# Strassen's scheme in the first layer of an expert FFN on one Trainium2 core: seven products in place of eight

## The chip, the core and the metric

The kernel runs on one core of a Trainium2 chip. TensorE (PE) multiplies matrices: it holds a stationary operand of 128x128, streams a moving operand past it and writes into PSUM. VectorE (DVE) and ScalarE (ACT) work on rows in SBUF and PSUM, GpSimd (POOL) on SBUF alone, SyncE (SP) issues DMAs. The metric is the device time of one execution in microseconds; the kernel before takes 1500.97 us, the median of three runs from 1498.53 to 1502.5.

## The reference

```python
# 1. attention: 4 x 8 heads, 768 steps, head size 40, a 40x40 state per head
y[t] = r[t] @ state
state = state * w[t] - (state @ a[t]) b[t] + v[t] k[t]
# 2. first FFN: x is 3072 x 320
x = (max(x @ w_in, 0) ** 2) @ w_out              # 320 -> 2048 -> 320
# 3. second FFN: 4 experts, every token goes to all of them
p = domain_probs / (domain_probs.sum(-1) + 1e-9)
out = sum over e of p[:, e] * (max(x @ w1[e], 0) @ w2[e])   # 320 -> 1024 -> 320
```

All is float32. The matmuls of the FFNs run on numbers of fewer bits (fp32r), so each operand is split into a rounded high part and a low part that is the rest; a product is made of three: high x high, high x low, low x high.

## The kernel before

The first half of the program is the attention, in 24 steps, with the first FFN beside it: 12 blocks of 256 tokens, each with 16 tiles of 128 hidden features. The order of all that is made by a list scheduler (`Schedule`) from operations with costs, due times and dependencies. Block 11 of the first FFN is written out behind it, by the list `ffn`: units (layer one of a tile) and ends (layer two), the end two tiles behind the unit. The results of a block go to DRAM (`y1d`, `y1_out`), with the last 64 of 320 features doubled on POOL (`y1_double`).

The second FFN runs over 4 experts, 12 blocks, 8 tiles of 128 hidden features: 384 items. Its input is loaded back from `y1d` (`x2_load`), transposed on PE and split by ACT and DVE (`x2_tr`, while block 11 and expert 0 run), and stays in SBUF for all experts (`x2h`, `x2l`). A tile's weights are loaded, rounded by ACT, and their low parts are made by DVE and POOL (`load_w`). An item is `ffn1`, 8 matmuls of 256 columns: 320 features are 128 + 128 + 64, three matmuls for each 128 and two for the 64, whose high and low weights share the partitions. ACT then makes the high part of the rectified result and DVE its low part (L1013, L1014); `ffn2` is 6 matmuls of 320 columns, one item later, so that PE doesn't wait for the two. After 8 items the result of a block is scaled by the token's probability and added up: by ACT for expert 0 (L995), by DVE for the others (L997). The last expert's blocks go out by SP (L999).

Each engine runs its instructions in the order of the program. PSUM has eight banks: two for layer one (`ps1`), two for transposes (`pst`), four for two blocks of layer two (`ps2`, `ps3`).

## Time and profile before

| | |
|---|---|
| three runs, median | 1500.97 us |
| the profiled execution | 1497.41 us |
| its span, first to last instruction | 1495.6 us |
| mean granted TensorE clock | 0.971 |
| busy: PE, PE weight loads | 1406.6, 1341.6 us |
| busy: DVE, ACT, POOL | 837.2, 736.6, 210.4 us |
| first and last L1013 (items of the second FFN) | 786.2, 1489.7 us |
| moved by DMA | 107.18 MB |

The span is the time from the first to the last instruction. Busy time is the union of an engine's instructions; PE's are pipelined, so a matmul's duration (0.28 us) is longer than the distance to the next one's start. "Idle before" is the time in which an engine stood still ahead of an instruction, and the arrow says what ended it.

### The profile page before, as it was taken

To read this page: it belongs to the slowest core of one execution; us is meant where nothing else is said; L and a number is where in the kernel's file an instruction comes from. 1 tells how busy PE (TensorE), PEld (TensorE's weight loads), DVE (VectorE), ACT (ScalarE), POOL (GpSimd) and SP (SyncE) were. 2 spreads that over 40 slices of the span, in tenths; PEclk is the share of its full clock that TensorE was granted. 3 is DMA by queue.
4 is the path that set the end of the run, shared out by engine and by line. 5 is a ranking of instruction groups with operands and counts; after the bars stand their busy time and mean duration, and the time that the engine had idled before them with its cause. 6 is when DMAs were issued, how large, how long until landed. Compare 5 with 4: busy or idle time off the path is not lost.

```text
span 1495.6 us, 39619 instructions
## 1 busy us (share of the span) xinstructions
PE 1406.6 (94%) x16336; PEld 1341.6 (90%) x16336; DVE 837.2 (56%) x2184; ACT 736.6 (49%) x1943; POOL 210.4 (14%) x299
## 2 busy tenths in 40 slices
PE   3788999899999999999999999999999999999998
PEld 3476889788888888888999999999999999999998
DVE  7889968778778778778443333233333333323322
ACT  5487768667677777677673333322222222222221
POOL 4121322221312312311020000000000000000000
PEclk9899989899999999999999999999999999999999
DMA  8465343342442442431141111000000000000000
GB/s 249 110 192 172 91 119 88 109 133 71 125 124 78 127 130 67 133 99 50 36 132 61 42 50 52 1 30 20 30 1 11 20 1 2 1 10 27 19 27 27
DMA packets 133909, 107.18 MB, mean 72 GB/s; under 512 B 95968, under 2 KB 108256, under 8 KB 133728
## 3 DMA queue, kind: packets, MB, share of 16 engines
q1 hardware_dynamic: 133728, 104.64, 24.6%
q8 instruction: 129, 2.11, 0.6%
q14 instruction: 52, 0.43, 0.1%
HBM read 85.34 MB, written 14.55 MB: 67 GB/s over the span
## 4 chain that ended last, share of the span: by engine, by line
PE 72%; DVE 10%; DMA 8%; ACT 5%; issue 2%; SPq 2%; POOL 1%; DVEq 0%; ACTq 0%; POOLq 0%
PE z L251 24%; PE h L251 8%; PE pz L257 8%; PE pz L260 8%; PE pz L256 8%; PE px L571 3%; PE py L260 3%; DMA td<-mu 2%; PE py L256 2%; DMA TT<-td 2%; DVE t L745 2%; PE py L257 2%; DVE tmp L742 2%; PE ptx L648 2%; DMA xr<-y 1%
## 5 line engine op out<-in xcount | busy, mean ns | idle before, releaser
L1014 DVE SCALAR_TENSOR_TENSOR zl<-z,zh 128x256 fp32r<-128x256 f32 x384 | 163.0, 424 | 466.2 <-ACT zh L1013 466.2
L1013 ACT ACTIVATE zh<-z 128x256 fp32r<-128x256 f32 x384 | 147.5, 384 | 506.6 <-PE z L251 505.0
L251 PE MATMUL z<-x2h,w 128*128 128x256 f32 x1920 | 380.8, 282 | 0.0
L251 PE MATMUL z<-x2l,w 128*128 128x256 f32 x1152 | 320.4, 278 | 0.0
L251 PEld LDWEIGHTS z<-x2h,w 128*128 128x128 f32 x1920 | 306.3, 188 | 0.0
L257 PE MATMUL pz<-w,zh 128*128 128x320 f32 x768 | 231.3, 309 | 0.0
L256 PE MATMUL pz<-w,zh 128*128 128x320 f32 x768 | 230.7, 308 | 0.0
L251 PEld LDWEIGHTS z<-x2l,w 128*128 128x128 f32 x1152 | 216.8, 188 | 0.0
L251 PE MATMUL h<-xh,w 128*128 128x256 f32 x960 | 198.1, 289 | 0.0
L260 PE MATMUL pz<-w,zl 128*128 128x320 f32 x768 | 175.0, 309 | 0.0
L251 PE MATMUL h<-xl,w 128*128 128x256 f32 x576 | 164.0, 286 | 0.7 <-DVE xl L872 0.7
L251 PEld LDWEIGHTS h<-xh,w 128*128 128x128 f32 x960 | 157.4, 193 | 2.2
L256 PEld LDWEIGHTS pz<-w,zh 128*128 128x128 f32 x768 | 144.4, 188 | 0.0
L257 PEld LDWEIGHTS pz<-w,zh 128*128 128x128 f32 x768 | 144.2, 188 | 0.0
L256 PE MATMUL py<-w,gh 128*128 128x320 f32 x384 | 127.6, 340 | 5.1 <-ACT gh L807 5.1
L812 DVE TENSOR_TENSOR gl<-r,gh 128x256 fp32r<-128x256 f32 x192 | 84.7, 442 | 78.0 <-ACT r L809 77.3
L260 PEld LDWEIGHTS pz<-w,zl 128*128 128x128 f32 x768 | 128.4, 188 | 0.0
L257 PE MATMUL py<-w,gh 128*128 128x320 f32 x384 | 118.5, 316 | 0.0
L251 PEld LDWEIGHTS h<-xl,w 128*128 128x128 f32 x576 | 111.2, 193 | 0.9 <-DVE xl L872 0.9
L804 ACT ACTIVATE r<-h 128x256 f32<-128x256 f32 x192 | 73.3, 382 | 63.7 <-PE h L251 54.9
L745 DVE TENSOR_TENSOR t<-t,tmp 128x126 f32<-128x126 f32 (+22 forms) x372 | 96.5, 259 | 6.8
L260 PE MATMUL py<-w,gl 128*128 128x320 f32 x384 | 93.7, 326 | 6.5 <-DVE gl L812 6.2
(104 smaller groups left out, 2305.7 us busy)
## 6 DMA issues: line engine op xcount, KB each, us to landing
in<-kba SPq DMA_DIRECT2D x24, 768.0 KB
raw<-wf SPq DMA_DIRECT2D x32, 352.0 KB
raw<-wm SPq DMA_DIRECT2D x32, 234.0 KB
wd<-w SPq DMA_DIRECT2D x24, 264.0 KB
rf<-rv SPq DMA_DIRECT2D x24, 256.0 KB
r<-rv SPq DMA_DIRECT2D x24, 256.0 KB
v<-rv SPq DMA_DIRECT2D x24, 256.0 KB
mu<-md SPq DMA_DIRECT2D x24, 256.0 KB
```

The source lines that it names most:

```text
L251: pe.matmul(ps, a, b, start=n == 0, stop=n == len(mm) - 1)
L256: pe.matmul(pys[tt], gh[:, sl], t[:, 256:576], start=first, stop=False)
L257: pe.matmul(pys[tt], gh[:, sl], t[:, 960:1280], start=False, stop=False)
L260: pe.matmul(pys[tt], gl[:, sl], t[:, 256:576], start=False, stop=last)
L571: pe.matmul(px[64 * j:64 * j + 64, p], t[:, 0:64], t[:, 64:168], start=True, stop=True)
L648: pe.matmul(d["ptx", h][own(h, j), p], T[i, 4 * h + p], d["x", h][i, p], start=True, stop=True)
L742: dve.tensor_tensor(v["tmp"], a, b, ALU.mult)
L745: dve.tensor_tensor(c, c, v["tmp"], ALU.subtract)
L804: act.activation(g["r"], g["ps"], AF.Relu)
L812: dve.tensor_tensor(g["gl"], g["r"], g["gh"].bitcast(F32), ALU.subtract)
L1013: act.activation(gh, ps, AF.Relu)
L1014: dve.scalar_tensor_tensor(gl, ps, 0.0, gh.bitcast(F32), ALU.max, ALU.subtract)
```

## The change

The second FFN works on pairs of blocks (512 tokens) and pairs of tiles (256 hidden features): 4 experts x 6 pairs x 4 = 96 steps. In a step layer one is a product of 2 x 2 blocks: two halves of the features (160 = 128 + 32), two of the hidden features (128), two of the tokens (256). Strassen's scheme, in Winograd's form, makes the four results out of seven products (`products`) in place of eight: each is four matmuls of 256 columns (high x high, high x low, low x high, and one for the 32 features that are left, with the parts beside each other on the partitions). The results are added up by DVE in a tile `C`, from PSUM, then rectified and split as before, with 512 columns an instruction. Layer two (`l2`, 24 matmuls of 320 columns) runs one step later.

The scheme wants four sums of the weights' blocks and four of the tokens', and the high and low parts of all seven operands. A planner (`Beside`) holds jobs with an engine, a duration, a due step and what they need, and at each step gives out jobs on each engine until a time for that engine is used up (`emit`); the times are 4.94 us of ACT, 3.19 of DVE, 3.87 of POOL and 3.0 of SP a step, and less beside block 11. Transposes (`x_block`) are given by `blocks`, at most two a step, inside `l2`. A pair's inputs are scaled by a power of two per token (`x2_big`, `x2_scale`, `x2_mul`), which the probabilities take back. The operands of the six pairs and of the sets of weights are made while block 11 and expert 0 run (experts 1 and 2 make the sets of the expert behind them), stored in DRAM by SP (`x_store`, `set_store`) and fetched by POOL's queue for the later steps (`x_fetch`, `set_fetch`). `load_w`, `x2_tr`, `y1_double` and the old loop go. Block 11's results go through DRAM like the others'.

```diff
-NF2 = 8
+NPAIR, NPW = 6, 4
...
+    def ready(self, j, n, eng):
+        _, _, _, _, _, _, deps, lag, after, _ = j
+        if n < after:
+            return False
+        for d in deps:
+            if d in self.jobs:
+                return False
+            if d in self.given:
+                at, by = self.given[d]
+                if by != eng and n < at + lag:
+                    return False
+        return True
...
+    def blocks(self, n, most):
+        while most:
+            l = sorted((j[:2], k) for k, j in self.jobs.items() if j[2] == ("pe",) and self.ready(j, n, "pe"))
+            if not l:
+                return
+            key = l[0][1]
+            j = self.jobs[key]
+            if j[9]:
+                most -= 1
+                eng = min(j[9], key=lambda e: self.used.get(e, 0))
+                self.used[eng] = self.used.get(eng, 0) + j[3]
+                self.give(key, n, eng, (self.engines[eng],))
+            else:
+                self.give(key, n, "pe")
...
+    def emit(self, n, budget):
+        left = {e: t - self.used.get(e, 0) for e, t in budget.items()}
+        while True:
+            l = []
+            for k, j in self.jobs.items():
+                for e in j[2]:
+                    if e in left and (left[e] > 0 or j[0] <= n) and self.ready(j, n, e):
+                        l.append((j[0], j[1], -left[e], e, k))
+            if not l:
+                break
+            _, _, _, e, k = min(l)
+            j = self.jobs[k]
+            left[e] -= j[3]
+            self.give(k, n, e, (self.engines[e],) if len(j[2]) > 1 or j[4].__name__ in ("x_round", "set_round", "set_round2") else ())
+        self.used = {e: -min(0, t) for e, t in left.items()}
...
-    def y1_double(k):
-        pool.tensor_copy(yy[k][:, :, 320:384], yy[k][:, :, 256:320])
+            yy[k] = buf3(f"y1_{k}", *buf)[:, 0:2 * DM].rearrange("p (c x) -> p c x", c=2)
+        act.copy(yy[k][:, t], py[k][t])
...
+    xsd = dram.tile([NPAIR, 128, 21 * 256], F32R, name="xsd", bufs=1)
+    wsd = dram.tile([NPW, 128, 31 * 128], F32R, name="wsd", bufs=1)
...
+        sp.dma_start(m.rearrange("p (c x) -> p c x", c=2)[:, :, 0:512], wf[n, :, 0:1024].rearrange("p (c x) -> p c x", c=2))
+        sp.dma_start(w, wf[n, :, 1024:1664])
...
+    def set_sum(n, o, x, y, f):
+        m = raw[n][0]
+        pool.tensor_tensor(m[:, :, o], m[:, :, x], m[:, :, y], f)
...
+    def set_round(s, i, eng):
+        m = flat(raw[s.n][0][:, i // 2])
+        h = slice(448 * (i % 2), 448 * (i % 2) + 448)
+        copy(eng, (s.a, s.b)[i // 2][:, h], m[:, h])
...
+    def set_low(s, i):
+        m = flat(raw[s.n][0][:, 0])
+        o = (s.b[:, 896:1280], s.a[:, 896:1280], s.l)[i]
+        h = slice(384 * i, min(384 * i + 384, 896))
+        minus(dve, o, m[:, h], f32(s.a[:, h]))
...
+    def set_rest(s):
+        c = flat(raw[s.n][0][64:96, 1])
+        minus(pool, c, c, f32(s.b[64:96, 0:896]))
...
+    def set_fetch(s):
+        for t, x, y in parts(s):
+            pool.dma_start(t, wsd[s.n % NPW, :, x:y])
+        slot[s.n] = s
...
+    def x2_mul(k):
+        for t in range(2):
+            y = yl[k][:, t, :, 0:160]
+            dve.tensor_scalar(y, y, inv[:, 2 * k + t:2 * k + t + 1], None, ALU.mult)
...
+        ps = pst.tile([128, 2, 2, 128], F32, tag="tr", name=f"ptr{p}_{i}")
+        for t in range(2):
+            y = yl[2 * p + k][:, t, h]
+            pe.transpose(ps[:, 0, t], y[:, 0:128], ident)
+            pe.transpose(ps[:, 1, t], y[:, 128:256], ident)
+        copy(eng, xc[p][:, :, o], ps.rearrange("p c t x -> p c (t x)"))
+
+    def x_sum(p, o, a, b):
+        r = xc[p]
+        minus(pool, r[:, :, o], r[:, :, a], r[:, :, b])
...
+        copy(eng, xs[0, p][:, o, 0:2], xc[p][:, :, o])
+
+    def x_low(p, o):
+        minus(dve, xs[0, p][:, o, 2], xc[p][:, 0, o], f32(xs[0, p][:, o, 0]))
+
+    def x_rest(p, o):
+        c = xc[p][32:64, 1, o]
+        minus(pool, c, c, f32(xs[0, p][32:64, o, 1]))
+
+    def x_done(p, o):
+        act.copy(xs[0, p][32:64, o, 1], xc[p][32:64, 1, o])
...
+    def x_store(p):
+        sp.dma_start(f32(xsd[p]), f32(xs[0, p].rearrange("p a b x -> p (a b x)")))
+
+    def x_fetch(e, p):
+        xs[e, p] = bp2.tile([128, 7, 3, 256], F32R, tag="X", name=f"X{e}_{p}")
+        pool.dma_start(xs[e, p].rearrange("p a b x -> p (a b x)"), xsd[p])
...
+        Q = [
+            (ps1 if i < 2 else pst).tile([128, 2, 256], F32, tag="l1" if i < 2 else "tr", name=f"Q{n}_{i}")
+            for i in range(4)
+        ]
+
+        def prod(i, q):
+            hi, c = v.a[:, 128 * i:128 * i + 128], v.b[:, 128 * i:128 * i + 128]
+            o = Q[q % 4][:, q // 4]
+            pe.matmul(o, hi, X[:, i, 0], start=True, stop=False)
+            pe.matmul(o, hi, X[:, i, 2], start=False, stop=False)
+            pe.matmul(o, v.low(i), X[:, i, 0], start=False, stop=False)
+            pe.matmul(o, c, X[:, i, 1], start=False, stop=True)
+            return o
+
+        C = bp.tile([128, 4, 256], F32, tag="C", name=f"C{n}")
+        c22, c12, c21, c11 = (C[:, i] for i in range(4))
+        plus = lambda o, x, y: dve.tensor_tensor(o, x, y, ALU.add)
+        g = gz[n] = {}
+
+        def relu(i, units):
+            gh, gl = low_home(n, 2 * i), low_home(n, 2 * i + 1)
+            src = C[:, 0::3] if i == 0 else C[:, 1:3]
+            act.activation(gh, src, AF.Relu)
+            for x, u in enumerate(units):
+                g[u] = gh[:, x], gl[:, x]
+            return lambda: dve.scalar_tensor_tensor(gl, src, 0.0, f32(gh), ALU.max, ALU.subtract)
+
+        act.copy(c11, prod(0, 0))
+        plus(c21, c11, prod(5, 1))
+        plus(c12, c21, prod(4, 2))
+        p7 = prod(3, 3)
+        plus(C[:, 0:3:2], C[:, 1:3], sub(p7, [[0, 2], [1, 256]]))
+        plus(c11, c11, prod(1, 4))
+        low = relu(0, ((1, 1), (0, 0)))
+        plus(c12, c12, prod(6, 5))
+        plus(c21, c21, prod(2, 6))
+        low()
+        relu(1, ((0, 1), (1, 0)))()
...
+        for t in range(4):
+            if t == 3 and hook:
+                hook()
+            sl = slice(128 * (t % 2), 128 * (t % 2) + 128)
+            for f in range(2):
+                gh, gl = g[f, t // 2]
+                hi, lo = w[:, 320 * f:320 * f + 320], w[:, 640 + 320 * f:960 + 320 * f]
+                pe.matmul(py2[0][t], gh[:, sl], hi, start=j == f == 0, stop=False)
+                pe.matmul(py2[0][t], gh[:, sl], lo, start=False, stop=False)
+                pe.matmul(py2[0][t], gl[:, sl], hi, start=False, stop=j == NPW - 1 and f == 1)
...
+        D = {0: (-51, -15, -14, -13, -11, -8, -6, -4, -4), 1: (-13, -9, -10, -8, -3, -3, -1, 1, 1)}.get(
+            P, tuple(e + d for d in (-8, -6, -5, -5, -4, -4, -2, -2, 0)))
+        ld = [job("sp", 0.45, x2_load, k + i, deps=[("blk", P - 1, 2 * i), ("blk", P - 1, 2 * i + 1)], lag=0, due=D[0], key=("ld", k + i)) for i in range(2)]
+        bg = [job("dve", 0.82, x2_big, k + i, deps=[ld[i]], lag=2 if P else 1, due=D[1]) for i in range(2)]
...
+            job("pe", 0.66, x_block, P, i, deps=free + [dup[i // 2]], due=D[4], key=("blk", P, i), via=("act", "dve") if P == 0 else ("act",))
...
+            raw_of[o] = job("pool", 1.33, x_sum, P, o, x, y, deps=blks, lag=0, due=D[5])
...
+            r = job(("act", "dve") if P == 0 else ("act",), 0.65, x_round, P, o, deps=[raw_of[o]], due=D[6], lag=0 if o in (0, 1, 6) else 1, after=NPW * (P - 1) - 1 if P else -99)
+            job("dve", 0.42, x_low, P, o, deps=[r], due=D[7], key=("low", P, o))
+            c = job("pool", 0.72, x_rest, P, o, deps=[r] + [raw_of[u] for u in users[o]], lag=0, due=D[7])
+            job("act", 0.41, x_done, P, o, deps=[c], due=D[8], key=("done", P, o))
+        job("sp", 0.45, x_store, P, deps=[(x, P, o) for x in ("low", "done") for o in range(7)], due=e + 4, after=e + 1)
...
+            b = PER * e + (0 if e == 0 else 1) + (6 if e == 0 else 2) * i
+            prev = prepare(Set(n, spare, b), tuple(b + d for d in (0, 2, 5, 1, 1)), b, ("act",), i < NPW - 1, prev)
...
+            at(post, PER * (e + 1) - NPW + i, set_fetch, Set(NPW * (e + 1) + i, homes[i - 1]))
+        homes, spare = [spare] + homes[:NPW - 1], homes[NPW - 1]
+    for G in range(NPAIR, NE * NPAIR):
+        at(post, NPW * (G - 2) + 3, x_fetch, *divmod(G, NPAIR))
...
+    light = dict(act=0.66, dve=1.22, pool=2.56, sp=2.0)
+    i = -NP
+    plan.emit(i - 1, light)
+    for g, k, f in ffn:
+        if g is moe1_end and f == NF1 - 1:
+            plan.must(0)
+            products(0, *steps[0])
+        g(k, f)
+        if g is moe1_unit and f < 2 or g is moe1_end:
+            plan.blocks(i, 2)
+            plan.emit(i, light)
+            i += 1
+    for n, s in enumerate(steps):
+        e, p, j = s
+        if n:
+            products(n, *s)
+            l2(n - 1, *steps[n - 1], lambda: plan.blocks(n, 2))
+            if j == 0:
+                l2_end(*steps[n - 1][:2])
         else:
...
+            plan.blocks(0, 2)
+        plan.emit(n, dict(act=4.94 - 2.1 * (e == j == 0), dve=3.19 - 2.1 * (e > 0 and j == 0), pool=3.87, sp=3.0))
+        run(post, n)
```

## Rows read from the trace of the kernel before

**Rows 1.** The page: busy us, share, instructions; then tenths in 40 slices.
```profile
PE 1406.6 (94%) x16336; PEld 1341.6 (90%) x16336; DVE 837.2 (56%) x2184; ACT 736.6 (49%) x1943; POOL 210.4 (14%) x299
...
PE   3788999899999999999999999999999999999998
...
DVE  7889968778778778778443333233333333323322
...
ACT  5487768667677777677673333322222222222221
...
PEclk9899989899999999999999999999999999999999
```

**Rows 2.** Windows of the second FFN: stretch, length, busy us, clock, DMA, GB/s.
```profile
800.00:820.00 20.00, 20.00 (x158) 19.99 (x157) 6.71 (x15) 8.13 (x19) 1.03 (x1) 1.00 0.13 39
...
1000.00:1100.00 100.00, 100.00 (x771) 100.00 (x771) 34.14 (x75) 25.13 (x61) 6.20 (x6) 1.00 0.07 23
```

**Rows 3.** PE in order of time, one item: start, duration in us, line, tiles.
```profile
801.23 0.28 PE L251 MATMUL z<-x2h,w 128*128 128x256 f32 x1
...
802.17 0.31 PE L256 MATMUL pz<-w,zh 128*128 128x320 f32 x1
...
803.05 0.82 PE L967 MATMUL ptr<-cs,yl 128*128 128x128 f32 x6
...
803.63 0.37 PE L251 MATMUL z<-x2h,w 128*128 128x256 f32 x1
```

**Rows 4.** Groups by line, DVE: shapes, count, busy us, mean ns, idle before.
```profile
L812 DVE TENSOR_TENSOR gl<-r,gh 128x256 fp32r<-128x256 f32 x192 | 84.7, 442 | 78.0 <-ACT r L809 77.3 <-ACT y L826 0.2
...
L536 DVE TENSOR_TENSOR xv<-pv,cs 64x512 f32<-64x512 f32 x96 | 64.2, 686 | 2.1 <-PE pv L531 0.3
...
L668 DVE TENSOR_TENSOR ys<-pys,FF 128x256 f32<-128x256 f32 x48 | 19.6, 409 | 0.0
...
L872 DVE TENSOR_TENSOR xl<-xr,xh 128x768 fp32r<-128x768 f32 x12 | 11.5, 957 | 2.6 <-ACT xh L869 1.4 <-ACT gh L807 0.5
```

**Rows 5.** Order of time, POOL and DVE early in the attention stage.
```profile
15.64 1.25 POOL L454 TENSOR_TENSOR in<-in,s 128x512 f32<-128x512 f32 x1 [0.66 <-DVE s L442]
...
15.73 1.30 DVE L306 TENSOR_SCALAR raw<-raw 128x236 uint32<-128x236 uint32 x1
...
17.14 0.39 DVE L308 SCALAR_TENSOR_TENSOR raw<-raw 128x236 uint32<-128x236 uint32 x1
...
17.46 0.27 DVE L306 TENSOR_SCALAR raw<-raw 128x234 uint32<-128x234 uint32 x1
```

**Rows 6.** One line of the inversion: durations in ns, shortest, median, longest.
```profile
L745 DVE TENSOR_TENSOR t<-t,tmp x372: 135/261/1192, 34.4 to 712.4; 128x126 f32<-128x126 f32 x18, 128x30 f32<-128x30 f32 x12, 128x56 f32<-128x56 f32 x12, 128x78 f32<-128x78 f32 x12
```

**Rows 7.** Groups by line, ACT and POOL.
```profile
L1013 ACT ACTIVATE zh<-z 128x256 fp32r<-128x256 f32 x384 | 147.5, 384 | 506.6 <-PE z L251 505.0
...
L683 POOL TENSOR_TENSOR y<-ys,q 128x256 f32<-128x256 f32 x48 | 37.4, 779 | 22.9 <-DVE ys L668 22.9
...
L446 POOL TENSOR_TENSOR in<-in,q 128x512 f32<-128x512 f32 x24 | 32.5, 1353 | 9.5 <-DVE q L442 5.5 <-ACT r L809 4.0
...
L548 ACT COPY kbt<-pk 128x512 f32<-128x512 f32 x48 | 27.5, 580 | 8.1 <-PE pk L544 8.1
...
L829 POOL COPY y<-y 128x128 f32<-128x128 f32 x12 | 5.2, 435 | 234.9 <-ACT y L826 234.9
```

**Rows 8.** PE in order of time at the last block of the first FFN.
```profile
754.75 0.31 PE L257 MATMUL py<-w,gh 128*128 128x320 f32 x1
...
756.84 0.56 PE L260 MATMUL py<-w,gl 128*128 128x320 f32 x2 [1.78 <-DVE gl L812]
```

**Rows 9.** Waits from 745 to 800 us: total, times, longest.
```profile
DVE psum__13043 L945 <- DMA prob<-dp: 4.4, 1, 4.4
```

**Rows 10.** Windows again: DMA share and GB/s in the last two columns.
```profile
0.00:100.00 100.00, 65.67 (x1003) 51.95 (x1004) 84.19 (x268) 59.38 (x180) 29.11 (x41) 0.90 0.64 185
...
10.00:20.00 10.00, 3.48 (x120) 3.24 (x124) 8.60 (x20) 3.57 (x12) 6.19 (x6) 1.00 1.04 325
...
755.00:760.00 5.00, 3.22 (x16) 3.16 (x16) 2.09 (x7) 1.26 (x4) 0.00 (x0) 0.73 0.97 329
```

More of the change, by code (lines that the diff above doesn't have):

```diff
@@ L843, in moe1_end @@
                 y1_copy(k, t)
[L844 to L846 removed]
+            y1_out(k)
     def moe1(k, tt):
@@ L1021 @@
+    l2(len(steps) - 1, *steps[-1])
+    l2_end(*steps[-1][:2])
+    assert not plan.jobs and not post, (plan.jobs, post)
 _INS = ["kba", "w", "rv", "vn", "wm", "wf", "dp", "cst"]
```

262 lines of the change are left out of this document (183 added, 79 removed).

## The prediction

> **What bounds the kernel now.** I read the page first [rows 1]: TensorE (PE) is busy 94% of a span of 1495.6 us, VectorE (DVE) 56%, ScalarE (ACT) 49%, GpSimd (POOL) 14%, and in the right half of the slice view PE stands at 9 and its clock at 9 while DVE falls to 3 and ACT to 2. Then the windows of the second FFN [rows 2]: 100.00 of 100 us busy at granted clock 1.00 (the 2.4 GHz level), DVE 34, ACT 25, POOL 6. No wait of another engine ends last there; matmuls do, one after the other. So in this stage time is the number of matmuls times their spacing, and what the other engines do is free until one of them is full.
>
> The spacing stands in the order of time of one item [rows 3]: eight matmuls of 256 columns from 801.23 to 802.17, 0.94/8 = 0.1175 us each; six of 320 columns from 802.17 to 803.05, 0.88/6 = 0.147 each; six transposes from 803.05 to 803.63, 0.097 each.
>
> **The change, part by part.**
>
> *Matmuls removed.* Four items (two token blocks, two tiles of 128 hidden features) were 4 x 8 = 32 matmuls of 256 columns and 24 of 320. One step of the new loop does the same work with 7 products x 4 = 28 and the same 24. There are 4 experts x 6 pairs x 4 = 96 steps: 96 x 4 x 0.1175 = 45.1 us less. A step is 28 x 0.1175 + 24 x 0.147 = 6.82 us of PE; this is the measure for all other engines below.
>
> *Transposes added.* 6 pairs x 16 = 96 in place of 72: 24 x 0.097 = 2.3 us more. PE's floor falls by 42.8 us. This sum holds while PE never waits.
>
> *DVE in a step.* Five additions of 256 columns out of PSUM (0.409, L668), one of 512 (0.686, L536), two subtractions of 512 with both inputs in SBUF: 0.42 for 256 and 0.957 for 768 (L812, L872) give 0.69 [rows 4]. Sum 2.05 + 0.69 + 1.38 = 4.1 us. After that come jobs, while expert 0 runs (steps 0 to about 20): per pair of blocks two reductions of 640 (0.82 by the slope of L812 and L872), five small operations (0.9), four multiplications of 320 (0.32 by the 0.27 for 234 in [rows 5]) and seven subtractions of 256: 1.6 + 0.9 + 1.3 + 2.9 = 6.7 us, that is 1.7 a step; per set of weights 384 + 384 + 128 + 320 + 320 columns, 2.4 us every six steps, 0.4 a step. Together 6.2 us. Durations overlap when operations follow each other: one of 0.39 starts at 17.14 and the next at 17.46 [rows 5], 0.07 less; for some 13 operations 0.9. So DVE needs 5.3 of 6.82 us, if it waits for nothing.
>
> *ACT in a step.* One copy of 256 (0.384, L1013) and two activations of 512 (0.58, by L548) are 1.5; per pair 4 copies and 7 roundings of 512 and 7 copies of 256, 9.1 us or 2.3 a step; weights 0.65; the scaling of the results 0.5 [rows 7]. 5.0 of 6.82: hidden.
>
> *POOL in a step.* Per pair four copies (0.44, L829), four sums of 512 (1.35, L446), seven subtractions of 256 (0.78, L683): 12.6 us, 3.2 a step; per set four sums of 256 and one of 896 columns, 5 us or 0.8 a step [rows 7]. 4.0 of 6.82: hidden by itself.
>
> *DVE and POOL together* are the one place where I expect something to be given back. A DVE operation of 0.27 us took 1.30 at 15.73, while a POOL operation ran from 15.64 to 16.89; the next ones of the same line and of its neighbour took 0.27 and 0.39 again [rows 5]. It waited out the other engine. The Trainium skill has the rule (page "SBUF — State Buffer", section "Who interferes with whom"): a DVE instruction with two SBUF inputs, or in a two-port mode, and a GpSimd instruction that reads SBUF take one port pair for their whole length, and whichever comes second blocks. The trace agrees (1.30 for 0.27).
> In the new loop about 6.3 DVE operations a step are of that kind (two subtractions, and a quarter of 7 + 4 + 4, and some of the weights'), and POOL is busy 4.0/6.82 = 0.58 of the time. An operation that arrives by chance waits 0.58 x half of about 0.9 us = 0.27 us. 6.3 x 0.27 = 1.7; DVE then needs 7.0 us against 6.82. Both ends: no waits at all give 5.3, nothing lost; a wait of 1.03 (1.30 - 0.27) for each gives 11.8, 5.0 too much, 100 us over 20 steps. I take 0.2 a step plus unevenness of jobs, 0.4 in all: 20 x 0.4 = 8 us. The chance arrival is nearer to the rows than the far end: of 372 subtractions on one line half took 0.26 us or less, the longest 1.19 [rows 6].
>
> *A pair's chain in expert 0.* Its blocks are transposed two a step, each pair's only once the pair before is ready; then POOL has four sums and seven subtractions, 5.4 + 5.5 us, with copies of ACT between and behind [rows 7]. From the second two blocks to the first product that reads them are two steps, 13.6 us. That leaves some 2 us, and a set's longest POOL operation (2 us) or waits on the port can take them: for each of the pairs 2 to 5 between 0 and 5 us of PE. I take 1 each, 4 us; the near end, as the slack is positive.
>
> *Experts 1 to 3* have no such jobs but one set of weights every two steps early on: DVE 4.1 + 0.5 (four scalings a pair) + 1.2 = 5.8 at the most, hidden. Products, additions and the second layer are one step apart: the chain behind the last product (one addition, an activation, two subtractions, some 2 us) lies beside the 24 matmuls of the step before, 3.5 us. DVE's last addition of a step ends some 3.9 us after the step's first matmul, and its bank is written again at 6.82 + 0.94: DVE may be 3.8 us late before PE waits.
>
> *The last block of the first FFN.* The old loop prepared eight tiles of weights and one block here; the new one prepares a pair, four sets and part of the next pair. In the trace PE loses 1.78 us at 756.84, behind a DVE operation that waits 4.4 us for the probabilities' DMA [rows 8, 9]; that code stays, and so does the clock of 0.73 in that stretch [rows 10], so I count no gain. New work needed before step 0: about 20 us on POOL (two blocks' copies, four sums, seven subtractions, two sets' sums), 11 on DVE and 14 on ACT, beside 16 x 0.42 and 16 x 1.2 of the first FFN, in some 30 us. Nothing overflows for sure; the loads may come late. Ends 0 and 8 us, the latter if step 0 waits for a pair that is one set's preparation (5 us of POOL, 3 of rest) late. I take 2.
>
> *DMAs.* A pair's operands are 128 x 21 x 256 x 4 B = 2.75 MB, a set 2.03 MB; both are stored during expert 0 and fetched again. At a change of expert two pairs and three sets, 11.6 MB, are due in 8 steps, 54.6 us: 212 GB/s, where the trace has 325 and 329 in full stretches and 185 as the mean of the first 100 us [rows 10]. At the first change a store of a pair and one of a set come on top: 16.4 MB, 300 GB/s. Hidden, with little room once; behind it the next pair's products would wait. Fetches are issued by POOL, which in the trace issues none, and each waits there for PE to be done with a buffer; what is queued behind is only the next sets' sums, due some steps later. Cost 0; other end in the rivals.
>
> *Small edits.* The copy that doubled 64 columns on POOL goes (12 x 0.44 us, with nobody near waiting) and block 11 goes through DRAM like the others; 0. The step's removal changes the list that orders the attention stage; its PE idles there anyway, so either sign is possible: 0, bounds 3 us each way.
>
> **Sum.** The profiled execution took 1497.4 us (span 1495.6 and 1.8 around it). 1497.4 - 45.1 + 2.3 + 8 + 4 + 2 = 1468.6. The three runs' median is 1501.0, 3.6 above the profiled one; for a median run I forecast 1472.
>
> **Rivals.**
>
> *1. Nothing is given back.* The jobs fall beside DVE's five reads of PSUM, which don't meet POOL, and PE stays full. For it: DVE's 5.3 leaves 1.5 us a step. Against it: POOL needs 4.0 and DVE's two-input work about 2.6, nearly the whole step for one port. 1501.0 - 42.8 = 1458. Chance 0.22.
>
> *2. Slower: the two engines block each other in expert 0.* If POOL always has work queued, each DVE operation with two inputs meets a running one. With 0.65 us each (half of 1.30) DVE needs 5.3 + 6.3 x 0.65 = 9.4 a step, 2.6 over PE; 20 steps give 52 us, and 1501.0 - 42.8 + 6 + 52 = 1516. It decides from 0.53 us a wait: (5.3 + 6.3 x 0.53 - 6.82) x 20 = 36, which with the 6 of chain and start eats the 42.8. For it: the 1.30 of [rows 5], and POOL four times as busy as in the mean of before; against it: both queues work in order and POOL runs out of work between pairs. Taken to the letter, the rule of the Trainium skill named above (page "SBUF — State Buffer") is this rival. Chance 0.14 (0.11 slower, 0.03 within).
>
> *3. The fetches don't come in time.* At 185 GB/s 11.6 MB take 62.7 us, 8 us late at two changes; 16.4 MB take 88.6, 34 late at the first: 1501.0 - 42.8 + 14 + 50 = 1522. It decides below about 200 GB/s; at 276 it is 5 us, once. For it: the mean of 185; against it: that stretch was not full (share 0.64), full ones have 325. Chance 0.08 (0.04 slower, 0.02 within, 0.02 faster).
>
> **How the numbers follow.** My forecast, part of the gain given back, has 0.56 (1461 to 1486). Within 0.3% of 1501.0, 4.5 us either way, is what a measurement can't tell from no change. Faster: 0.56 + 0.22 + 0.02 = 0.80; within: 0.03 + 0.02 = 0.05; slower 0.11 + 0.04 = 0.15. For 8 in 10 the range goes from 1455 (rival 1 less the 3 us of the attention stage) to 1494 (a part of rivals 2 and 3).
>
> **What would show it.** PE matmul counts lower by 384 and higher by 24; steps of experts 1 to 3 of 6.82 us at clock 1.00; in expert 0 gaps of PE that end on a DVE addition or on an operand of the products, some 12 us in all; DVE subtractions there longer than 0.42, POOL's longer than 0.73. Wrong: a wait of PE on a DMA at a change of expert (rival 3), gaps of 2 us in every step of expert 0 (rival 2), a period in experts 1 to 3 above 6.9, or a stage before step 0 longer by more than 8 us.

## The result: 0.6% slower, and the profile after

The changed kernel took 1508.6 us in the median of 17 runs, beside 1498.1 for the kernel before on the same chip: ratio 1.006, 95% interval 1.0041 to 1.008. Forecast were 1472 us and a range of 1455 to 1494.

Lines of its page (those of before are in [rows 1], but for POOL's slices):

```profile
span 1507.5 us, 39913 instructions
PE 1385.9 (92%) x15976; PEld 1313.5 (87%) x15976; DVE 1133.4 (75%) x2721; ACT 807.9 (54%) x1990; POOL 367.9 (24%) x479
...
PE   3698999999999899999986989999999999999999
...
DVE  7899978778778778767389777766776677766665
...
POOL 4121331222222221311076344531221212110000
PEclk9889999899899999889997999999999999999999
```

The 360 matmuls fewer are there (384 less, 24 more), and PE's right quarter stands at 9. The loss is in the middle: the slices 21 and 22 of PE (754 to 829 us) are 8 and 6, its clock falls to 7 in the second, and there DVE stands at 8 and 9 and POOL at 7 and 6, its highest.

Windows of the changed kernel: the last block of the first FFN, then steps 0 to 3, then 100 us of expert 3 (length, busy us of PE, PEld, DVE, ACT, POOL, clock, DMA share, GB/s):

```profile
749.00:796.00 47.00, 38.66 (x259) 36.17 (x260) 37.75 (x70) 29.34 (x71) 29.79 (x36) 0.93 0.34 111
796.00:838.00 42.00, 30.04 (x194) 29.27 (x193) 38.99 (x72) 21.17 (x43) 22.55 (x19) 0.80 0.31 109
...
1346.00:1446.00 100.00, 100.00 (x765) 100.00 (x764) 63.03 (x130) 24.20 (x44) 2.11 (x4) 1.00 0.32 119
```

Expert 3 is what [rows 2] showed before: PE 100 of 100 us at clock 1.00, DVE risen from 34 to 63. In steps 0 to 3 DVE is busy 38.99 of 42 us, PE 30.04, at a granted clock of 0.80. What PE waited for in the changed kernel from 750 to 1500 us (total, times, longest):

```profile
PE Q L1203 <- DVE C L1211: 12.1, 13, 3.1
PE Q L1205 <- DVE w L1013: 11.8, 2, 7.2
PE py L317 <- DVE gl L869: 6.8, 5, 2.6
PE Q L1203 <- ACT C L1222: 6.4, 5, 1.6
PE Q L1204 <- DVE X L1013: 1.5, 1, 1.5
```

Before, only 2.5 us of waits stood in that stretch. The whole list of after, these five lines and three shorter ones, adds up to 40 us, and none of its lines names a DMA.

I cut the time at four places of the trace: the first matmul of the last block after its wait on ACT, the first product, and ACT's copies that begin steps 4 and 24 (and 48, 72). All stages in us; "floor" is the matmuls' spacing with the transposes, for the last block the time of before (34.9) plus 2.5 us of transposes. Each row is one profiled run: in kernels without the interleaving that differ only in due steps or in POOL's pieces, steps 4 to 23 came out between 164.0 and 166.2 us, so a difference of 2 us there decides nothing.

| kernel (profiled run) | last block | steps 0-3 | steps 4-23 | experts 1+2 |
|---|---|---|---|---|
| floor | 37.4 | 27.2 | 142.2 | 326.4 |
| changed kernel | 46.6 | 42.5 | 165.8 | 333.6 |
| rest on DVE | 41.9 | 50.1 | 177.9 | 334.5 |
| POOL writes only | 40.7 | 38.4 | 158.2 | 326.6 |
| interleaved | 46.6 | 44.4 | 155.5 | 333.6 |
| both of these | 40.7 | 40.0 | 154.0 | 326.7 |
| rest on DVE, interleaved | 42.1 | 51.4 | 166.0 | 331.3 |
| earlier sets alone | 47.0 | 40.2 | 164.0 | 333.7 |
| order of all | 46.8 | 39.9 | 166.2 | 333.7 |
| rest in four alone | 45.7 | 42.9 | 165.3 | 332.2 |
| low parts on ACT | 47.6 | 39.0 | 168.4 | 333.6 |
| interleaved, earlier sets | 46.5 | 40.4 | 157.9 | 333.6 |
| the same, rest in four | 46.1 | 41.4 | 155.6 | 326.9 |
| the same, sums in two | 47.0 | 41.8 | 157.9 | 327.0 |
| rest in four, done later | 46.1 | 40.9 | 156.6 | 327.0 |
| the same, rounds at step 0 | 45.9 | 41.8 | 157.7 | 327.0 |
| the same, rounds at step 1 | 46.0 | 42.7 | 156.4 | 327.0 |

Expert 3 takes 170 us in all of them. (The attention stage ahead ended between 742.6 and 756.3 us in these runs, so I compare stages, and whole kernels by their ratios.) The changed kernel gives back 9.2 + 15.3 + 23.6 + 7.2 = 55 us, more than the 43 that it saves: 55 - 43 = 12, and its profiled run is 1507.5 - 1495.6 = 11.9 us longer. The waits are 40 of the 55; the rest lies in the matmuls themselves, which follow each other more slowly behind a wait (0.23 us for 0.12 behind the one at 848.52) and where the granted clock was lower (0.80 in the second window).

### The profile page after: what moved, and what is told of

Same layout as the page of the kernel before. It is cut to its first block, busy times and chain, and to the rows that moved or that the text cites. A ratio compares the mean times of both kernels' runs of the same rounds, so it can differ in the third digit from the quotient of the medians.

```text
span 1507.5 us, 39913 instructions
## 1 busy us (share of the span) xinstructions
PE 1385.9 (92%) x15976; PEld 1313.5 (87%) x15976; DVE 1133.4 (75%) x2721; ACT 807.9 (54%) x1990; POOL 367.9 (24%) x479
## 4 chain that ended last, share of the span: by engine, by line
PE 55%; DVE 19%; ACT 8%; DMA 8%; issue 5%; SPq 3%; POOL 1%; DVEq 0%; ACTq 0%
PE pz L1250 7%; PE pz L1251 7%; PE pz L1249 7%; PE Q L1203 5%; PE Q L1206 4%; PE Q L1205 4%; PE Q L1204 4%; PE h L308 4%; DVE t L802 3%; DVE tmp L799 3%; DVE gl L869 2%; PE px L628 2%; DMA td<-mu 2%; DMA TT<-td 2%; PE ptx L705 2%
## 5 line engine op out<-in xcount | busy, mean ns | idle before, releaser
L1211 DVE TENSOR_TENSOR C<-C,Q 128x256 f32<-128x256 f32 (+1 forms) x576 | 242.6, 461 | 193.0 <-PE Q L1206 141.1
L1217 ACT ACTIVATE z<-C 128x512 fp32r<-128x512 f32 x192 | 121.5, 633 | 247.9 <-DVE C L1211 245.3
L1249 PE MATMUL pz<-w,z 128*128 128x320 f32 x768 | 238.6, 311 | 0.0
L1250 PE MATMUL pz<-w,z 128*128 128x320 f32 x768 | 238.0, 310 | 0.0
L1251 PE MATMUL pz<-w,z 128*128 128x320 f32 x768 | 238.0, 310 | 0.0
L1203 PE MATMUL Q<-X,w 128*128 128x256 f32 x672 | 193.1, 287 | 18.7 <-DVE C L1211 12.1
L1204 PE MATMUL Q<-X,w 128*128 128x256 f32 x672 | 189.8, 282 | 1.5 <-DVE X L1013 1.5
L1206 PE MATMUL Q<-X,w 128*128 128x256 f32 x672 | 190.0, 283 | 0.2 <-ACT w L1092 0.2
L1205 PE MATMUL Q<-X,w 128*128 128x256 f32 x576 | 163.4, 284 | 11.8 <-DVE w L1013 11.8
L1203 PEld LDWEIGHTS Q<-X,w 128*128 128x128 f32 x672 | 128.1, 191 | 22.7 <-DVE C L1211 15.0
L869 DVE TENSOR_TENSOR gl<-r,gh 128x256 fp32r<-128x256 f32 x192 | 94.9, 494 | 69.8 <-ACT r L866 51.9
L1220 DVE SCALAR_TENSOR_TENSOR z<-C,z 128x512 fp32r<-128x512 f32 x192 | 143.6, 767 | 3.8
L1249 PEld LDWEIGHTS pz<-w,z 128*128 128x128 f32 x768 | 145.2, 189 | 0.0
L1250 PEld LDWEIGHTS pz<-w,z 128*128 128x128 f32 x768 | 145.1, 189 | 0.0
L1251 PEld LDWEIGHTS pz<-w,z 128*128 128x128 f32 x768 | 144.7, 188 | 0.0
L1222 ACT COPY C<-Q 128x256 f32<-128x256 f32 x96 | 35.8, 373 | 183.1 <-PE Q L1206 182.8
L313 PE MATMUL py<-w,gh 128*128 128x320 f32 x384 | 127.6, 340 | 4.8 <-ACT gh L864 4.8
L1204 PEld LDWEIGHTS Q<-X,w 128*128 128x128 f32 x672 | 128.1, 191 | 1.7 <-DVE X L1013 1.7
L1206 PEld LDWEIGHTS Q<-X,w 128*128 128x128 f32 x672 | 128.3, 191 | 0.5 <-ACT w L1092 0.5
```

Of the source, the lines that this page charges most:

```text
L313: pe.matmul(pys[tt], gh[:, sl], t[:, 256:576], start=first, stop=False)
L869: dve.tensor_tensor(g["gl"], g["r"], g["gh"].bitcast(F32), ALU.subtract)
L1203: pe.matmul(o, hi, X[:, i, 0], start=True, stop=False)
L1204: pe.matmul(o, hi, X[:, i, 2], start=False, stop=False)
L1205: pe.matmul(o, v.low(i), X[:, i, 0], start=False, stop=False)
L1206: pe.matmul(o, c, X[:, i, 1], start=False, stop=True)
```

## Experiments

Letters that the expectations use: P, a DVE operation with two SBUF inputs waits out a POOL operation that reads SBUF; L, DVE has more work before step 3 than time; B, two products share a PSUM bank, so PE waits as soon as DVE or ACT is some 1 us late; Q, POOL's own chain for a pair is too long; O, work that is ready stands in a queue behind jobs that are needed later. Ratios are to the kernel before; the changed kernel's is 1.006.

**Rest on DVE.** POOL's subtractions for the last 32 features move to DVE:

```
-        minus(pool, c, c, f32(xs[0, p][32:64, o, 1]))
+        minus(dve, c, c, f32(xs[0, p][32:64, o, 1]))
...
-        minus(pool, c, c, f32(s.b[64:96, 0:896]))
+        minus(dve, c, c, f32(s.b[64:96, 0:896]))
...
-            c = job("pool", 0.72, x_rest, P, o, deps=[r] + [raw_of[u] for u in users[o]], lag=0, due=D[7])
+            c = job("dve", 0.42, x_rest, P, o, deps=[r] + [raw_of[u] for u in users[o]], lag=0, due=D[7])
...
-        c = job("pool", 2.2, set_rest, s, deps=r[2:] + m, lag=0, due=D[3])
+        c = job("dve", 1.1, set_rest, s, deps=r[2:] + m, lag=0, due=D[3])
```

> The 42 subtractions x_rest (32x256) and the 13 set_rest (32x896) move from POOL to DVE, planned there at 0.42 and 1.1 us. DVE gets 42 x 0.42 + 13 x 1.1 = 32 us more work, POOL loses 42 x 0.9 + 13 x 2.1 = 65 us that read SBUF. Theory P (a DVE operation with two SBUF inputs waits out a POOL operation that reads SBUF): the DVE subtractions x_low fall from 0.77 us in the mean to 0.42 to 0.5, set_low2 from 0.89 to 0.5, and the time falls by 5 to 20 us, to 1489 to 1503. Theory L (DVE has too many jobs around step 0, whatever POOL does): DVE's stretch before step 3 gets longer by 14 x 0.42 + 4 x 1.1 = 10 us, the time goes to 1515 to 1525. Theory B (PE waits because two products share a PSUM bank): experts 1 to 3 keep their eight steps of 7.69 us or lose some of them, as set_rest no longer meets set_low2.

Measured 1524.8 us, 1.0162 [1.0116, 1.0209]: L's number. DVE's durations fell as P had said: from 750 to 1400 us the low parts of x took 0.496 us in the mean for 0.767, those of 320 columns of w 0.484 for 0.889, and the last block took 41.9 us for 46.6. But the work costs DVE more than its waits did.

**POOL writes only.** In place of the same subtractions POOL does memsets that read nothing (those features' low part is left out):

```
-        minus(pool, c, c, f32(s.b[64:96, 0:896]))
+        [pool.memset(c, 0.0) for _ in range(2)]
...
-        minus(pool, c, c, f32(xs[0, p][32:64, o, 1]))
+        [pool.memset(c, 0.0) for _ in range(3)]
```

> POOL's x_rest and set_rest are replaced by memsets of the same rows, three of 256 and two of 896 columns, which take about as long but read nothing; what is left out is the low part of the last 32 features. DVE and the order of the program stay as they are. Theory P: x_low takes 0.42 to 0.5 us, gl beside block 11 0.42 and not up to 2.3, and the time falls by 15 to 35 us, to 1474 to 1494. Theory L, or a POOL chain that is too long (theory Q): DVE's durations may change, the time stays within 5 us of 1508.

Measured 1484.3 us, 0.9898 [0.9848, 0.9948]: as P expected. The stages add up: 5.9 + 4.1 + 7.6 + 7.0 = 24.6 us, and 1.006 - 0.9898 is 24 us. From 750 to 1400 us POOL spends 37.1 us on the tokens' part for 36.9 in the changed kernel and 27.3 on the weights' for 34.4, and PE's wait on a pair's operands is 1.5 us in both; this speaks against a shorter chain of POOL as the cause. The DVE groups from 750 to 1400 us show the mechanism; first the changed kernel, the low parts of x and of w (shapes, count, busy us, mean ns):

```profile
L1013 DVE TENSOR_TENSOR X<-xc,X 128x256 fp32r<-128x256 f32 x42 | 30.1, 767 | 0.0
L1013 DVE TENSOR_TENSOR w<-wr,w 128x320 fp32r<-128x320 f32 x26 | 22.3, 889 | 0.0
```

and with POOL writing only:

```profile
L1013 DVE TENSOR_TENSOR X<-xc,X 128x256 fp32r<-128x256 f32 x42 | 17.2, 463 | 0.0
L1013 DVE TENSOR_TENSOR w<-wr,w 128x320 fp32r<-128x320 f32 x26 | 13.9, 569 | 0.0
```

In order of time in the changed kernel, pair 1's seven low parts; POOL has its own seven operations up to 816.25 and reads on behind them (start, us):

```profile
809.94 6.31 POOL L1013 TENSOR_TENSOR xc<-xc,X 32x256 f32<-32x256 f32 x7
...
812.99 7.48 DVE L1013 TENSOR_TENSOR X<-xc,X 128x256 fp32r<-128x256 f32 x7
```

and the same seven where POOL only writes (until 815.04, then it stands still):

```profile
814.41 2.43 DVE L1013 TENSOR_TENSOR X<-xc,X 128x256 fp32r<-128x256 f32 x7
```

7.48 us against 2.43 for one and the same work. PE's waits show where this counts; with POOL writing only the list from 750 to 1500 us begins:

```profile
PE Q L1203 <- ACT C L1222: 6.4, 5, 1.6
PE Q L1203 <- DVE C L1211: 6.2, 4, 2.3
...
PE Q L1205 <- DVE w L1013: 2.1, 2, 1.1
PE py L317 <- DVE gl L869: 2.1, 2, 1.4
```

The waits on DVE fell from 12.1, 11.8 and 6.8 to 6.2, 2.1 and 2.1 us. The 6.4 us on ACT's copy did not change: they are another loss. The fifth product goes into the bank of the first, which ACT copies out (L1222), and five times in expert 0 that copy stood in ACT's queue behind scalings and roundings. In the changed kernel:

```profile
844.97 1.79 ACT L1258 ACTIVATE acc<-pz,prob 128x320 f32<-128x320 f32 x4
...
848.11 0.36 ACT L1222 COPY C<-Q 128x256 f32<-128x256 f32 x1
...
848.52 0.39 PE L1203 MATMUL Q<-X,w 128*128 128x256 f32 x1 [1.36 <-ACT C L1222]
```

**Interleaved.** Half of the second layer of the step before goes between the fourth and the fifth product, so that DVE and ACT have 1.8 us more before a bank is written again:

```
-        plus(c11, c11, prod(1, 4))
+        if mid:
+            mid()
+        plus(c11, c11, prod(1, 4))
...
-            products(n, *s)
-            l2(n - 1, *steps[n - 1], lambda: plan.blocks(n, 2))
+            products(n, *s, mid=lambda: l2(n - 1, *steps[n - 1], ts=range(2)))
+            l2(n - 1, *steps[n - 1], lambda: plan.blocks(n, 2), ts=range(2, 4))
```

> Half of layer two's matmuls of the step before (12 of 24) stand between the fourth and the fifth product; nothing else changes. The fifth product writes the bank that the first one's reader still reads, and so on: this gives DVE and ACT 1.8 us more there. Theory B: the eight steps of 7.69 us in experts 1 and 2 go to 6.80 (7 us), and the waits of about 1 us in most steps from 4 to 17 of expert 0 (some 14 us of gaps) shrink; the time falls by 10 to 20 us, to 1489 to 1499. Theories P and L alone: DVE is the bound where PE waits, so the gaps move to another place and the time stays within 5 us of 1508; the 12 us of waits for weights at steps 1 and 2 stay under every theory.

Measured 1498.5 us, 1.0002 [0.997, 1.0035], at the upper end of what B expected. 10 us of steps 4 to 23 come back, and nothing before or behind them. Of PE's waits there, the 6.4 us on ACT's copy are gone, those on DVE's additions fell from 7.6 to 4.2, and those on a pair's operands rose from 1.5 to 4.9. The eight steps of experts 1 and 2 that B had named are a miss: they still lose 7.2 us. One of them:

```profile
1025.53 0.28 PE L1203 MATMUL Q<-X,w 128*128 128x256 f32 x1
...
1027.07 2.12 POOL L1013 TENSOR_TENSOR wm<-wm,w 32x896 f32<-32x896 f32 x1 [8.96 <-ACT w L1010]
...
1027.54 2.41 DVE L1013 TENSOR_TENSOR w<-wr,w 128x320 fp32r<-128x320 f32 x2
...
1030.33 0.38 PE L1203 MATMUL Q<-X,w 128*128 128x256 f32 x1 [0.54 <-DVE C L1211]
```

POOL's operation now begins 1.54 us behind the step's first matmul, where it began 0.19 ahead of it (rows of 1037 below), and DVE's low parts wait for its end: DVE is later by as much as the interleaving gave.

**Rest on DVE, interleaved.** Both edits together.

> Both edits of the two runs before. If P and B are both at work and apart (P in the stretch before step 3, B after it), the gains add up: 15 to 40 us less, 1469 to 1494, below the kernel before. If they are one and the same cause seen twice, this is no better than the better one of the two.

Measured 1509.5 us, 1.0078 [1.0051, 1.0104]: a miss, worse than interleaving alone. The slack does not make room for DVE's extra work.

**Both of POOL writes only and interleaved.** The low part of the last 32 features is left out here too.

> Both single changes together: POOL's subtractions for the last 32 features replaced by memsets that read nothing (the low part of those features is left out), and half of the second layer between the fourth and fifth product. If port waits (P) and the PE waits on shared PSUM banks (B) are separate losses, their gains of 24 and 10 us against the changed kernel add up: 1470 to 1478 us. If they are one loss seen from two sides (PE waits in the banks only because DVE was held up by POOL), the second adds little to the first: 1481 to 1486.

Measured 1485.9 us, 0.9909 [0.9882, 0.9936], no better than POOL writing only, so the two gains do not add up; that they are one loss seen from two sides is only partly so. In steps 4 to 23 they give 7.6 and 10.3 us alone and 11.8 together: ACT's 6.4 us go here too, which POOL writing only had left. But steps 0 to 3 take 1.6 us more, and the waits on a pair's operands are 5.2 us for 1.5.

**Interleaved, earlier sets.** Due steps of sets 1 and 2:

```
-(-8, -9, -2, -1, -1), (-6, -1, 0, 0, 1)
+(-8, -9, -3, -3, -2), (-6, -1, -1, -1, 0)
```

> Interleaved as before, and the due steps of sets 1 and 2 are set earlier (low parts of set 1 due at step -2 instead of -1, of set 2 at 0 instead of 1), so that on DVE they stand ahead of pair 1's low parts, which are needed only at step 4. Theory L (DVE simply has more jobs between 770 and 823 us than time, and those of pair 1 stand ahead of those needed first): the two waits on the sets' low parts, 4.56 and 8.26 us in the interleaved kernel, fall by half or more, and nothing is late at step 4 by as much: 1486 to 1493 us. Theory P alone (what DVE loses is the waiting on POOL, whichever job stands first): the gap moves to step 4 and the time stays, 1496 to 1500.

Measured 1493.9 us, 0.997 [0.9933, 1.0006]: between the two. The waits on the low parts went, others of 3.75 and 4.11 us came in steps 1 and 2, ended by ACT.

**The same, rest in four.** A set's last rows in four POOL instructions:

```
-        minus(pool, c, c, f32(s.b[64:96, 0:896]))
+        for h in range(0, 896, 224):
+            minus(pool, c[:, h:h + 224], c[:, h:h + 224], f32(s.b[64:96, h:h + 224]))
```

> As the interleaved kernel with the earlier due steps, and the one 2.1 us POOL subtraction of a set's last rows in four pieces of 224 elements. Theory P in its exact form (a DVE instruction with two SBUF operands waits for the end of the one POOL instruction that runs, and no longer): the two low parts of w in experts 1 and 2 take some 1.4 us for 2.0, their eight PE gaps of 0.54 us go (steps back at 6.80), with 1 to 3 us more in expert 0: 5 to 8 us under the kernel without the pieces. If DVE instead waits until POOL's whole row of reads is over, nothing changes (within 1.5 us); if what matters is POOL's total time reading, too.

Measured 1490.3 us, 0.9926 [0.9896, 0.9956]: 6.6 us less by the ratios, and as much in experts 1 and 2 (333.6 to 326.9), where the steps are back at 6.81 in the mean.

**The same, sums in two.** POOL's four sums of a pair in halves.

> As the kernel with the pieces, and POOL's four Strassen sums of a pair (1.42 us each, 512 elements) in halves of 256 elements. Theory P: a low part of x beside a sum takes about 0.8 us for 1.48; 3 to 6 us less than with the set's pieces alone. Theory Q (POOL's own chain of a pair is what the steps wait for): the halves cost POOL more fixed time, and the waits on a pair's last operands grow: the same or up to 4 us more.

Measured 1495.0 us, 0.9968 [0.9952, 0.9984]: 6 us more by the ratios, 4 by the stages: near Q's number, but not by Q's way. POOL's sums took 36.1 us for 31.9 between 742 and 1004 us and the low parts of x 0.680 for 0.733, but the waits on a pair's operands did not grow (4.7 us for 4.9). What cost the time stays open.

**Rest in four alone**, in the changed kernel.

> The changed kernel with one edit: a set's last rows in four POOL pieces. Theory P in its exact form: the eight steps of 7.69 us in experts 1 and 2 fall back to 6.80 (7.1 us), and up to 4 us in expert 0 and before it: 1497 to 1502 us. If the low parts were late for another reason than the length of one POOL instruction: 1506 to 1510.

Measured 1505.6 us, 1.0035 [1.0008, 1.0061]: a miss; the steps of 7.69 fell to 7.52 only. So neither the pieces nor the interleaving clears the eight waits alone (332.2 and 333.6), and both together do (326.9). In order of time, first the changed kernel:

```profile
1037.08 2.11 POOL L1013 TENSOR_TENSOR wm<-wm,w 32x896 f32<-32x896 f32 x1 [8.98 <-ACT w L1010]
...
1037.27 0.28 PE L1203 MATMUL Q<-X,w 128*128 128x256 f32 x1
...
1037.93 2.01 DVE L1013 TENSOR_TENSOR w<-wr,w 128x320 fp32r<-128x320 f32 x2
1039.87 2.71 DVE L1211 TENSOR_TENSOR C<-C,Q 128x256 f32<-128x256 f32 x6
...
1039.50 0.28 PE L1206 MATMUL Q<-X,w 128*128 128x256 f32 x1
1040.33 0.38 PE L1203 MATMUL Q<-X,w 128*128 128x256 f32 x1 [0.56 <-DVE C L1211]
```

then the one with four pieces:

```profile
1030.70 2.79 POOL L1013 TENSOR_TENSOR wm<-wm,w 32x224 f32<-32x224 f32 x4 [8.53 <-ACT w L1010]
...
1032.02 1.83 DVE L1013 TENSOR_TENSOR w<-wr,w 128x320 fp32r<-128x320 f32 x2
```

The two operations take 1.83 us for 2.01: each now waits out a piece of its own (0.96 and 0.95 us, for 0.48 undisturbed). So "one instruction, and no longer" holds for each DVE operation, but a row of pieces meets a row of operations. The rows show the bank as well: the last matmul of the fifth product starts at 1039.50, and the sixth, into the other half of the tile that the second one filled, only at 1040.33, when the first of the additions, some 0.42 us from 1039.87 on, has read the second.

**Earlier sets alone**, in the changed kernel.

> The changed kernel with one edit: the due steps of sets 1 and 2 earlier, so that their low parts stand ahead of pair 1's on DVE. The gain that this had beside the interleaving was 5 us; order alone as a cause (L): 1500 to 1505. If it only moves the wait from the low parts to ACT's queue: 1506 to 1510.

Measured 1503.8 us, 1.0029 [1.0006, 1.0052]: within the number for order as a cause, though its interval overlaps the changed kernel's; and the waits that are left, 3.73 and 5.89 us at steps 0 to 1, are on ACT's queue, as the rival said.

**Low parts on ACT.** The low parts of x of pairs 0 and 1 are zeros written by ACT (left out, for their first 128 features):

```
     def x_low(p, o):
+        if p < 2:
+            act.mul(xs[0, p][:, o, 2], xc[p][:, 0, o], 0.0)
+            return
```

> The changed kernel with the 14 low parts of x of pairs 0 and 1 taken off DVE: ACT, which is busy a third to two thirds of the time there, writes zeros in their place (the low parts of those two pairs' first 128 features are left out). POOL is as before. They took DVE 13.8 us between 750 and 835 us. Theory L (DVE's queue before step 3 is the bound of that stretch): 10 to 15 us less, 1493 to 1499. Theory P alone (POOL's reads delay whatever DVE does): at most 3 us less, 1505 to 1509. If the chain of pair 0 (load, scale, transposes, sums) sets the start: the first product no earlier than 795.

Measured 1510.6 us, 1.0077 [1.0051, 1.0103]: no gain, against L's 10 to 15 us. Steps 0 to 3 took 3.5 us less, the last block 1.0 more and steps 4 to 23 2.6 more. The work went to ACT, and steps 1 and 2 now wait for it; its order of time in this kernel:

```profile
798.29 3.74 ACT L1010 CAST X<-xc 128x512 fp32r<-128x512 f32 x7
802.05 0.94 ACT L1092 CAST w<-acc 32x896 fp32r<-32x896 f32 x1
```

and PE's:

```profile
803.04 0.58 PE L1209 MATMUL Q<-X,w 128*128 128x256 f32 x1 [5.17 <-ACT w L1092]
```

The end of set 1, needed at step 1, stands behind seven roundings for step 4. That gave theory O.

**Done later**, in the kernel with the rest in four: the copy that ends sets 1 and 2 one step later.

> As the kernel with the set's last rows in four pieces, but the ACT copy that ends a set (L1093) is due one step later for sets 1 and 2, so that on ACT it stands behind the first copy of the next step's products. In the kernel before this one ACT stood 4.75 us at 795.5 to 800.2 for POOL's pieces with that copy behind it (two PE gaps of 4.9 and 2.7 us ended by it). If the queue of ACT is what these gaps cost: 4 to 7 us less, 1483 to 1487 us. If DVE's load there is the bound anyway (theory L), PE meets the next DVE job instead: 1488 to 1492.

Measured 1486.9 us, 0.9915 [0.989, 0.994]; that can't be told from 0.9926. A wait of 7.25 us was left, the one of the next expectation.

**Rounds later**, at step 0 and at step 1 instead of -1:

```
-1: (-13, -9, -10, -8, -3, -3, -1, 1, 1)
+1: (-13, -9, -10, -8, -3, -3, 0, 1, 1)
```

> As the kernel before with pair 1's roundings due at step 0 instead of -1. In that kernel ACT rounds pair 1's seven X tiles at 795.8 to 801.1 us, some of them while they wait for POOL's sums, and the copy that ends set 1 (its POOL rows were ready at 794.3) stands behind them until 801.1; PE waits 7.25 us for it. Theory O (what is late at steps 1 and 2 is ready in time and stands in a queue behind work for step 4): that gap falls to 2 us or less, 1480 to 1484 us. Theory L (too much work on DVE or ACT before step 3 whatever the order): the wait comes back at steps 2 to 5 in the same size, 1485 to 1489.

Measured 1490.9 us, 0.9946 [0.9927, 0.9966], above O's number and above L's.

> The same with pair 1's roundings due at step 1. Theory O: set 2's copies come free of them too (its gap of 1.1 us), 0 to 3 us less than at step 0: 1478 to 1483. If pair 1's own chain is then too late for step 4: a new gap there, and 2 to 6 us more than at step 0.

Measured 1492.8 us, 0.9959 [0.9941, 0.9977]: not O's number, and not to be told from step 0.

**Order of all**, in the changed kernel.

> The changed kernel with changes of due steps alone: sets 1 and 2 earlier, pair 1's roundings at step 0 for -1; no pieces, no interleaving. Theory O: the two gaps of 3.73 and 5.89 us at steps 0 to 1 that the earlier sets alone left (ended by ACT, on which a set's last copy stood behind other work) shrink by half or more: 1497 to 1501 us. Theory L: no change from 1503.8 within 2 us.

Measured 1508.0 us, 1.0061 [1.0037, 1.0085], 4 us more than the earlier sets alone, which neither theory had (the intervals overlap); the two gaps of 3.73 and 5.89 us became 3.74 and 3.69.

Theory O falls. With the rounds later the wait of 7.25 us is 2.1, but the stretch is no shorter; PE's waits in that kernel from 750 to 1000 us:

```profile
PE Q L1204 <- DVE C L1212: 7.7, 8, 2.9
...
PE Q L1207 <- ACT w L1093: 2.1, 1, 2.1
```

What went from one queue came in another, which is L's side, though L's numbers were too low. In no kernel did steps 0 to 3 take less than 38.4 us for 27.2.

## Why the prediction was wrong

The forecast gave back 14 us, the chip 55. Of the 41 between, 22.5 lie in the last block and steps 0 to 3 (24.5 us for 2), 11.6 in the rest of expert 0 (23.6 for the 8 + 4) and 7.2 in experts 1 and 2, which had no term. Two of the prediction's own signs of being wrong came: a stage before step 0 longer by more than 8 us (46.6 for 34.9) and periods above 6.9 us in experts 1 and 2 (eight of 7.69).

*Matmuls removed, transposes added: right.* The count is 360 lower, and the steps of expert 3 and of the undisturbed kernels take 6.80 us for 6.82. PE's floor fell by what was worked out.

*DMAs: right.* PE waits for none at a change of expert; rival 3 falls. A pair's fetch lands in 9.8 us:

```profile
X<-xsd POOLq DMA_DIRECT2D x18, 2688.0 KB, 9.8
```

*DVE and POOL together: the mechanism right, its price not.* A wait of 0.27 us for each of 6.3 operations a step was forecast, 34 us of DVE's time in 20 steps. The low parts of x took 0.767 us for 0.42, 0.35 more each; those of 320 columns of w 0.889 for 0.48. A wait is longer than forecast, but fewer operations meet one; the row of 372 subtractions [rows 6], which I took as a sign of chance arrivals, mixes shapes from 30 to 126 columns, so its median tells little of waits. In steps 4 to 23 the changed kernel and the one where POOL's last rows only write have the same 243 operations of DVE (length, busy us of PE, PEld, DVE, ACT, POOL, clock, DMA share, GB/s):

```profile
838.12:1003.92 165.80, 150.12 (x1106) 147.41 (x1105) 120.74 (x243) 85.00 (x176) 76.13 (x88) 0.98 0.51 189
...
831.89:990.07 158.18, 146.42 (x1106) 144.36 (x1105) 110.31 (x243) 85.12 (x176) 73.27 (x148) 1.00 0.53 199
```

That is 10 us of DVE's time for the 34 (POOL's sums still read in the second). And DVE is busy 120.74 of 165.80 us, so it was not full. What failed is how DVE's lateness becomes PE's: I let it cost only where DVE's mean rose over 6.82 us a step (0.4 a step, 8 us). With the port waits taken away 24 us came back, 13 of them in the last block and in experts 1 and 2, which had no such term.

*"DVE may be 3.8 us late before PE waits" is the step that failed.* I counted from DVE's last addition to the next step's use of its bank. The 3.9 us to that addition were right (1406.13 + 2.73 - 1404.92 in the rows below). But the products share banks two by two within a step: the sixth goes into the bank of the second, and starts 2.35 us (5 x 4 x 0.1175) after the first. In an undisturbed step of expert 3, from its first matmul on PE:

```profile
1404.92 0.28 PE L1203 MATMUL Q<-X,w 128*128 128x256 f32 x1
```

and DVE's row with the first additions:

```profile
1406.13 2.73 DVE L1211 TENSOR_TENSOR C<-C,Q 128x256 f32<-128x256 f32 x6 [2.32 <-PE Q L1206]
```

the first addition begins 1.21 us after the step and ends some 0.42 later, so the slack (how late DVE may be before PE waits) is 2.35 - 1.63 = 0.7 us. A set's two low parts are enough to break it: they take 2.01 us at 1037.93 and 0.88 where POOL doesn't read:

```profile
793.50 0.88 DVE L1013 TENSOR_TENSOR w<-wr,w 128x320 fp32r<-128x320 f32 x2
```

The first addition then begins 2.60 us after the step's first matmul and not 1.21, 1.39 late, and the sixth product 0.71 late (1040.33 for 1037.27 + 2.35). The trace shows it eight times in experts 1 and 2, which I had called hidden; with POOL writing only all eight steps are 6.80 or 6.81. ACT has the same short slack: in the undisturbed step its copy begins at 1405.59 and takes 0.37, and the fifth product, into the bank that the copy reads, starts at 1404.92 + 1.88, 0.8 us behind its end. I had called ACT hidden by its mean too, and its copy cost the 6.4 us in expert 0. So the runs show two causes: POOL's reads, 24 us of the 55, some at this slack and some ahead of step 4, and ACT's queue, 6.4 us of waits that its copy ended at this slack. Interleaving, which lengthens the slack, brought back 10 us from both. (PE's wait is one that the program sets. The Trainium skill, page "PSUM — Partial Sum Buffer", section "PSUM bank collisions raise a hardware error", tells to guard PSUM by bank and quadrant, not by address. The trace agrees in that the program waits by bank, 0.56 us at 1040.33 for a product into the other half; what would happen without the wait no run here shows.)

*The last block and the start, 2 us with ends 0 and 8: mis-sized.* They gave back 9.2 us in the last block and 15.3 in steps 0 to 3. I had added up each engine's new work (20, 11 and 14 us in some 30, beside 16 subtractions of the first FFN) up to step 0 only, and spread what comes behind over 20 steps. But sets 1 to 3 and pair 1 are due before step 4, and POOL's reads fall on most of it: DVE is busy 76.7 of the 89 us from 749 to 838. PE's two longest waits there, 4.55 and 7.25 us, are on low parts of sets 1 and 2, and the longest of the last block is on a low part of the first FFN that waited out POOL:

```profile
783.04 2.14 POOL L1013 TENSOR_TENSOR wm<-wm,w 32x896 f32<-32x896 f32 x1
...
783.17 2.29 DVE L869 TENSOR_TENSOR gl<-r,gh 128x256 fp32r<-128x256 f32 x1
...
785.51 0.83 PE L317 MATMUL py<-w,gl 128*128 128x320 f32 x2 [2.58 <-DVE gl L869]
```

In the stretch where PE stands most its granted clock is lower too, 0.80 from 796 to 838 us. That 6 us of the last block are port waits is shown (46.6 to 40.7). Which of the rest of steps 0 to 3, 11 us or more in every kernel, is DVE's work, POOL's or ACT's stays open: less work on DVE with more on ACT did not shorten the whole, nor did any order of the jobs (last block and steps 0 to 3 together took 86.6 to 89.1 us in these kernels, for 64.6 of floor); less of all three at once was not tried.

*A pair's chain, 4 us:* right in kind. The waits on a pair's operands were 1.5 us in the changed kernel and 4.3 to 5.2 in the interleaved ones.

*Rivals.* Rival 2 (the two engines block each other) is nearest to what happened: without POOL's reads of the last rows the kernel is faster than before (0.9898). But its number, 1516 for 1508.6 measured, is near by luck: it put 52 us into steps 0 to 19 by DVE's mean, where the port waits cost 24 us, 13 of them outside expert 0, and the rest has other causes. It was to decide from 0.53 us a wait, and 0.35 to 0.41 were enough beside the other losses, since slack and not the mean decides. I held it at 0.14, because "POOL runs out of work between pairs"; ahead of step 4 it seldom does (its slices of 7 and 6), and in experts 1 and 2, where it does, one operation of 2.11 us at the wrong place was enough.

*A version that beats both kernels.* Interleaved, with the earlier sets, the rest in four and the copy later: 1486.9 us, ratio 0.9915 [0.989, 0.994], with nothing of the computation left out. It is the best of several that were tried, and can't be told from the one without the later copy (0.9926).

## What to carry to other kernels

When work moves from PE to DVE, look for the first place in a step where a buffer or bank is used again, and take the slack there, for each engine that reads it, not over the step's mean; a burst of jobs costs its whole lateness beyond that slack. Count DVE's operations with two SBUF inputs against POOL's reading operations where both are dense, not over the span; and at the point where one stage hands over to the next, add up the work of both for each engine. If a job is late in one queue, moving it only helps when some engine has room at that time.
